# Gate matmuls, balancing rounds and attention spread out beside the products of a mixture-of-experts kernel

## The chip, the cores and the metric

The kernel runs on one core of a Trainium2 chip. The metric is the device time of one execution in microseconds (us). The core has five engines that run side by side, each with a queue of its own that it works off in order: TensorE (PE in the rows; its weight loads are PEld), VectorE (DVE), ScalarE (ACT), GpSimd (POOL) and SyncE (SP), which here only issues transfers. TensorE writes to PSUM, a memory of eight banks, which VectorE and ScalarE empty. Semaphores order the engines among each other. TensorE's clock has two levels, 1.2 and 2.4 GHz; the profile shows the granted share of the full one, 0.50 or 1.00.

## The reference

Three parts follow each other. `x` is 4 x 8 x 512 x 64, `state` 4 x 8 x 32 x 64; the tokens of both make N = 2176 rows of 512.

```python
# attention: x reads state, state reads x
a  = softmax(scale * x @ state.T);   xread = a @ state
a2 = softmax(scale * state @ x.T);   sread = a2 @ x
x  = concat([xread, sread], axis=2)  -> (2176, 512)

# first mixture of experts: all 8 experts for all rows, weights P balanced over rows and columns
logits = x @ w_gate
P = exp(logits - logits.max())
for _ in range(8):
    P /= P.sum(1) + 1e-9
    P /= P.sum(0) + 1e-9
    P *= N / E
out = sum over e of P[:, e:e+1] * (relu(x @ w1[e]) @ w2[e])      # w1[e] 512x1024, w2[e] 1024x512

# second: each row goes to one expert (argmax), scaled by its softmax weight and a sigmoid
```

The balancing needs the logits of all rows before its first round, and the expert sum needs its result, so the kernel of before already begins with unweighted sums.

## The kernel before

All of the change lies in the first two parts. The rows form 17 tiles of 128 (tiles 0 to 15 are `xread`, tile 16 is `sread`), and the products of the first mixture run in three passes of six, six and five tiles. A pass has 32 steps `s`: eight experts times four quarters of the hidden size (`FQ` = 256). A step is split in two halves. `mm1(s)` computes the hidden quarter for all tiles of the pass by seven block products of a fast matrix scheme (42 matmuls of 384 columns, since each value is split in a high and a low part and three partial products are taken). `mm2(s)` multiplies that with the second weights, tile by tile (six matmuls of 512 columns a tile), and adds the result to the tile's accumulator `acc` on VectorE. The program order on TensorE is mm1(0), mm1(1), mm2(0), mm1(2), mm2(1), and so on: `mm2(s-1)` stands behind `mm1(s)`.

The order of everything is written out by hand (`manual_schedule`). Batches 0 and 1 of attention are computed ahead of the first step, in a prologue. All other small work sits in a list, `queue`, of closures. Between the products `pump(dt)` adds `dt` (1.04 behind each of the seven block products, 1.36 behind each tile of `mm2`, about their time in us) to a credit, and takes the next item off the list each time the credit reaches `pace`. So `pace` is the distance between items in us of products, and an item's matmuls go into TensorE's queue at that place, its other instructions into the queues of their engines. `flush()` issues all that is left at once.

In the kernel of before the list holds, in this order: three gate batches for tiles 0 to 3, 4 and 5, 6 and 7; the items of batches 2 and 3 of attention (`window(2)`, `window(3)`, which also hold the state-reads-x part of batches 0 and 1, and end with a gate batch of four tiles each); the state-reads-x part of batches 2 and 3; the gate of tile 16. These 52 items have a pace of 66/52 = 1.27. Then `close_reads` releases attention's memory, sets the pace to 2.4, and the balancing follows: s0, s1, and eight rounds of two items, `row` and `col(i)`. At step 9 whatever is left is flushed and the routing constants are made on GpSimd. A gate of one tile is four matmuls with 8 columns (each two records in the trace, for the two halves of a 4-byte product), whose 128 x 128 stationary operand is the tile.

While the weights of the balancing aren't known, experts 0 and 1 are summed raw: expert 0 in `acc`, expert 1 in `xst` (the six tiles' transposed x, not needed any more by then). In the first quarter of expert 2 (`u == 2 * NQ`, `mm2(8)`, which stands in step 9's place behind mm1(9)) each tile's accumulator is scaled by its weight for expert 0, the raw sum of expert 1 is added with its weight, and the product of expert 2 with its own. From there on each eviction is one VectorE operation (`scalar_tensor_tensor`).

`load_x`, `load_state`: transfers of attention's inputs, the first on SyncE's queue, the second on ScalarE's, behind a memset on VectorE. `load_state(2)` and `load_state(3)` are issued just ahead of the first step, behind the splits of the first tiles. `state_T(b)` transposes the state of a batch on TensorE; it is the first item of `window(b)`. `prep_w1`, `prep_w2` split the next weights in high and low parts on ScalarE and GpSimd.

Lines of the kernel before that the rows below name: L137 `load_state`'s transfer, L166 `state_T`, L195, L206, L231, L243 attention's x-reads-state matmuls, L257, L272, L281 those of state-reads-x, L303 gate, L328 to L332 `row`, L337 to L341 `col`, L432 the low parts of the summed first weights, L465 to L467 `mm1`, L527 to L529 `mm2`, L541 and L542 the scaling and the merge of expert 1, L547 the weighted eviction.

Of the kernel before, what the change touches and what calls it, by code (L numbers as in the profile page):

```python
# [15 lines left out]
ALU = mybir.AluOpType  # L16
# [5 lines left out]
def tile_state_attention_moe_moe2(  # L22
# [13 lines left out]
    nc = tc.nc  # L36
    B, H, S, D = x.shape
    NS = state.shape[2]
    N, DM = out.shape
# [271 lines left out]
    def sinkhorn():  # L311
        steps = []
        mx, dg, ng = small([P, 1]), small([P, P]), small([P, 1])
        rs, rr = small([P, NT]), small([P, NT])
        cp, cr = small([P, E]), small([P, E])

        def s0():
            nc.vector.tensor_reduce(out=mx, in_=L1, axis=AX.XY, op=ALU.max)
            nc.vector.tensor_scalar_mul(dg, ident, mx)

        def s1():
            ps = bank("psmx")
            nc.tensor.matmul(ps[:, 0:P], ones, dg, start=True, stop=True)
            nc.vector.tensor_reduce(out=ng, in_=ps[:, 0:P], axis=AX.X, op=ALU.max, negate=True)
            nc.scalar.activation(out=PG, in_=L1, func=AF.Exp, bias=ng)

        def row():
            nc.vector.tensor_reduce(out=rs, in_=PG, axis=AX.X, op=ALU.add)  # L328
            nc.vector.tensor_scalar_add(rs, rs, EPS)
            nc.vector.reciprocal(rr, rs)  # L330
            nc.vector.tensor_tensor(out=PG, in0=PG, in1=rr.unsqueeze(2).to_broadcast([P, NT, E]), op=ALU.mult)
            nc.vector.tensor_reduce(out=cp, in_=PG.rearrange("p t e -> p e t"), axis=AX.X, op=ALU.add)  # L332

        def col(i):
            def f():
                ps = bank(f"pscol{i}")
                nc.tensor.matmul(ps[:, 0:E], ones, cp, start=True, stop=True)  # L337
                nc.vector.tensor_scalar_add(cr, ps[:, 0:E], EPS)
                nc.vector.reciprocal(cr, cr)
                nc.vector.tensor_scalar_mul(cr, cr, float(N) / E)  # L340
                nc.vector.tensor_tensor(out=PG, in0=PG, in1=cr.unsqueeze(1).to_broadcast([P, NT, E]), op=ALU.mult)  # L341
            return f

        steps += [s0, s1]
        for i in range(8):
            steps += [row, col(i)]
        return steps


# [166 lines left out]
    def accv(t):  # L516
        return acc[:, t % 6, :]

    def mm2(s, t):
        p, u = divmod(s, NU)  # L520
        e, q = divmod(u, NQ)
        hh, hl = hbuf(s)
        whi, wlo = W2[s]
        ps = bank(f"py{s}_{t}")
        r = slice((t - PASSES[p][0] // P) * P, (t - PASSES[p][0] // P + 1) * P)
        for j in range(2):
            nc.tensor.matmul(ps, hh[:, j, r], whi[:, j, :], start=(j == 0), stop=False)  # L527
            nc.tensor.matmul(ps, hh[:, j, r], wlo[:, j, :], start=False, stop=False)  # L528
            nc.tensor.matmul(ps, hl[:, j, r], whi[:, j, :], start=False, stop=(j == 1))  # L529
        a = accv(t)  # L530
        if p == 0 and e < 2:

            if e == 1:
                a = xst[:, t * DM : (t + 1) * DM]
            if q == 0:
                nc.vector.tensor_copy(a, ps)
            else:
                nc.vector.tensor_tensor(out=a, in0=ps, in1=a, op=ALU.add)
            return
        if p == 0 and u == 2 * NQ:  # L540
            nc.vector.tensor_scalar_mul(a, a, PG[:, t, 0:1])  # L541
            nc.vector.scalar_tensor_tensor(out=a, in0=xst[:, t * DM : (t + 1) * DM], scalar=PG[:, t, 1:2], in1=a,  # L542
                                           op0=ALU.mult, op1=ALU.add)
        if p > 0 and u == 0:
            nc.vector.tensor_scalar_mul(a, ps, PG[:, t, 0:1])
        else:
            nc.vector.scalar_tensor_tensor(out=a, in0=ps, scalar=PG[:, t, e : e + 1], in1=a, op0=ALU.mult, op1=ALU.add)  # L547
# [325 lines left out]
    with tc.manual_schedule():  # L873
# [57 lines left out]
        def flush():  # L931
            while queue:
                queue.pop(0)()
# [7 lines left out]
        def seq(*fs):  # L941
            def f():
                for g in fs:
                    g()
            return f

        def window(b):

            c, e = crit[b, 0], crit[b, 1]
            (n10, n20, n30), (n11, n21, n31) = lag[b - 2, 0], lag[b - 2, 1]  # L950

            def nx(g, f):
                def h():
                    f()
                    if b + 1 < B:
                        load_x(b + 1, g)
                    else:
                        load_x(b - 1, g)
                return h
            return [lambda: state_T(b), c[0], seq(lambda: load_x(b - 2, 0), n10), e[0], seq(lambda: load_x(b - 2, 1), n11),  # L960
                    c[1], n20, e[1], c[2], n21, e[2], c[3], nx(0, n30), e[3],
                    nx(1, n31), c[4], e[4], gate(range(4 * b, 4 * b + 4))]

        home = [None]

        def close_reads():
            actx.close()
            rtp[0] = ctx.enter_context(tc.tile_pool(name="rtp", bufs=1, side="right", reuse_waits="tile"))
            RT["oh"] = rtp[0].tile([P, NT, E], BF, name="oh")
            RT["bk"] = rtp[0].tile([P, NT], F32, name="bk")  # L970
            RT["g"] = rtp[0].tile([P, 2, NT], FR, name="gsplit")
            smp[0] = rtp[0]
            pace[0] = 2.4
            raw2 = ctx.enter_context(tc.tile_pool(name="raw2", bufs=1, side="right", reuse_waits="tile")).tile(
                [P, 4096], F32, name="raw2")
            R2[1], R2[2], R2[3] = raw2[:, 0:2048], raw2[:, 2048:4096], raw2[:, 0:2048]
            home[0] = raw2
            fin[0] = xctx.enter_context(tc.tile_pool(name="fin", bufs=2, side="right", reuse_waits="tile"))
            ohp[0] = xctx.enter_context(tc.tile_pool(name="ohp", bufs=1, side="right", reuse_waits="tile"))
# [39 lines left out]
                    f()  # L1019


        queue += [gate(range(0, 4)), gate(range(4, 6)), gate(range(6, 8))]
        for g in range(G):
            load_x(2, g)
        load_state(2)
        load_state(3)
        queue += window(2) + window(3)
        (a0, a1, a2), (b0, b1, b2) = lag[2, 0], lag[2, 1]
        queue += [a0, b0, a1, b1, seq(a2, lambda: load_x(3, 0)), seq(b2, lambda: load_x(3, 1))]
        (a0, a1, a2), (b0, b1, b2) = lag[3, 0], lag[3, 1]  # L1030
        queue += [a0, b0, a1, b1, a2, b2, seq(gate(range(NT - 1, NT)), states_out)]
        pace[0] = 66.0 / len(queue)
        queue += [close_reads] + sinkhorn()

        for s in range(3 * NU):
            p, u = divmod(s, NU)
            if s == 9:
                flush()
                routing_constants()
            if p < 2 and u == 14:  # L1040
                xload(p + 1)
            if p < 2 and u == 24:
                sums, T0 = xsums(p + 1, home[0])
                queue += sums
                pace[0] = 4.0
            if s == NU + 1:
                queue += list(Rq[0])
                pace[0] = 3.0
            if s == 2 * NU + 1:
                queue += [Rq[1][0], seq(Rq[1][1], sel_a), Rq[1][2], Rq[2][0], sel_b, sel_c, Rq[2][1], load_first, first_rows, Rq[2][2]]  # L1050
                pace[0] = 4.0
            step_mm1(s)
            if u < NU - 1:
                if u > 0:
                    step_mm2(s - 1)
                continue
            flush()
            ts = list(tiles_of(p))
            if p < 2:

                todo += xsplit(p + 1, T0)
                step_mm2(s - 1)
                hooks = {ts[i]: [A[ts[i - 1]]] + ([Bq[ts[i - 2]]] if i > 1 else []) for i in range(1, 6)}
                step_mm2(s, hooks)
                while todo:
                    todo.pop(0)()
                queue += [seq(A[ts[5]], Bq[ts[4]]), Bq[ts[5]]]
                pace[0] = 2.0
            else:
                load_first_raw(0, 0)  # L1070
                for i in (2, 3, 0, 1):
                    todo.append(lambda i=i: split_piece(SETS[0], i, 1024, nc.gpsimd))
                todo.append(lambda: load_first_raw(1, 1))
                step_mm2(s - 1)
                step_mm2(s, {13: [A[12]], 14: [A[13], Bq[12]], 15: [A[14], Bq[13]], 16: [Bq[14], A[15], lambda: xT(0)]})
# [142 lines left out]
```

## Time and profile before

| what | value |
|---|---|
| median of 3 runs (lowest to highest) | 1878.95 us (1878.01 to 1881.89) |
| the profiled execution: its time / its span | 1879.49 us / 1877.8 us |
| mean granted clock of TensorE | 0.973 |
| TensorE busy | 1804.5 us, 96% |
| VectorE / ScalarE / GpSimd busy | 65% / 35% / 59% |
| transfers | 154.65 MB, mean 82 GB/s |

Times of rows count from the span's start. A row of the timeline gives start, duration, engine, line, operation, output and inputs, the number of like instructions that follow each other, and in brackets the idle time of the engine before it with what ended it. Matmuls overlap, so the distance from one start to the next is the price of a matmul, not its duration. A row of the stretches gives the stretch and its length, the busy us (and instructions) of PE, PEld, DVE, ACT and POOL, the mean granted clock, the share of the transfer engines and GB/s. A row of the groups gives all instructions of a line and form.

### The profile page before, as it was taken

The numbers are of one execution on the slowest core, as the hardware profiler recorded it, in microseconds if no ns is written. First come the engines' busy times: TensorE is split into PE (matmuls) and PEld (weight loads), VectorE is DVE, ScalarE is ACT, GpSimd is POOL, SyncE is SP. The second block draws the span as 40 slices with busy tenths as digits, with TensorE's granted clock in tenths as the row PEclk, the third lists the DMA queues.
The fourth block names the chain that finished last, engine by engine and source line by source line (L and its number), as shares of the span: only waits on it lengthen the run. The fifth ranks groups of instructions, "written<-read, shape, count | busy, mean of one in ns | idle before, by whom it ended". The sixth has DMA issues, their size and how long they took to land.

```text
span 1877.8 us, 25502 instructions
## 1 busy us (share of the span) xinstructions
PE 1804.5 (96%) x9327; PEld 1607.7 (86%) x9327; DVE 1211.8 (65%) x2041; ACT 653.3 (35%) x1114; POOL 1099.3 (59%) x857
## 2 busy tenths in 40 slices
PE   7998899999999999999999999799999999899998
PEld 5997788999999889999999998689999899778886
DVE  5664769666666676666666666896666666745332
ACT  3432222333333333333333333333333343345333
POOL 2432456666776566666667765577787877412212
PEclk8799899999999999999999999899999999999999
DMA  4243112322222222222222222232222222245122
GB/s 113 74 107 96 51 45 68 102 68 68 68 68 68 90 80 71 70 71 96 68 68 68 68 67 84 67 129 81 80 79 79 90 79 68 76 137 199 62 81 89
DMA packets 126618, 154.65 MB, mean 82 GB/s; under 512 B 41424, under 2 KB 91600, under 8 KB 123920
## 3 DMA queue, kind: packets, MB, share of 16 engines
q1 hardware_dynamic: 121920, 142.41, 24.2%
q0 software_dynamic: 3280, 10.23, 1.7%
q8 instruction: 75, 1.23, 0.3%
q14 instruction: 63, 0.52, 0.1%
q10 hardware_dynamic: 1280, 0.26, 0.1%
HBM read 138.99 MB, written 14.42 MB: 82 GB/s over the span
## 4 chain that ended last, share of the span: by engine, by line
PE 74%; DVE 9%; issue 9%; DMA 5%; POOL 2%; ACT 1%; SPq 0%; POOLq 0%; DVEq 0%; ACTq 0%
PE py L527 12%; PE py L528 12%; PE py L529 12%; PE p L465 11%; PE p L467 11%; PE p L466 11%; DMA out_dram<-xst,si 4%; DMA out_dram<-y,si 1%; DVE HB L478 1%; PE psg L303 1%; PE psr L281 1%; PE pss L206 1%; PE pl L576 1%; DVE acc L547 1%; PE pso L243 1%
## 5 line engine op out<-in xcount | busy, mean ns | idle before, releaser
L443 POOL TENSOR_TENSOR wl<-rawb,wh 128x1024 fp32r<-128x1024 f32 x96 | 230.8, 2405 | 473.1 <-ACT wh L442 473.1
L465 PE MATMUL p<-XR 128*128 128x384 f32 (+1 forms) x1344 | 447.9, 333 | 4.2 <-ACT XR L390 2.8
L467 PE MATMUL p<-XR 128*128 128x384 f32 (+1 forms) x1344 | 444.1, 330 | 4.1 <-POOL XR L432 3.0
L466 PE MATMUL p<-XR 128*128 128x384 f32 (+1 forms) x1344 | 443.7, 330 | 0.9 <-DVE XR L392 0.9
L527 PE MATMUL py<-wh,HB 128*128 128x512 f32 x1088 | 431.6, 397 | 2.4 <-DVE acc L547 2.3
L528 PE MATMUL py<-wl,HB 128*128 128x512 f32 x1088 | 429.0, 394 | 0.0
L529 PE MATMUL py<-wh,HB 128*128 128x512 f32 x1088 | 428.6, 394 | 0.0
L547 DVE SCALAR_TENSOR_TENSOR acc<-py,PG,acc 128x512 f32<-128x512 f32 x485 | 338.9, 741 | 79.3 <-PE py L529 78.7
L432 POOL TENSOR_TENSOR XR<-sst,XR 128x1024 fp32r<-128x1024 f32 x96 | 255.0, 2656 | 50.8 <-ACT XR L426 50.8
L465 PEld LDWEIGHTS p<-XR 128*128 128x128 f32 x1344 | 256.8, 191 | 11.3 <-ACT XR L390 4.1
L467 PEld LDWEIGHTS p<-XR 128*128 128x128 f32 x1344 | 256.5, 191 | 5.4 <-POOL XR L432 3.8
L466 PEld LDWEIGHTS p<-XR 128*128 128x128 f32 x1344 | 256.7, 191 | 4.9 <-DVE XR L392 1.5
L478 DVE SCALAR_TENSOR_TENSOR HB<-u,HB 128x384 fp32r<-128x384 f32 (+1 forms) x192 | 169.3, 883 | 117.4 <-ACT HB L474 117.2
L529 PEld LDWEIGHTS py<-wh,HB 128*128 128x128 f32 x1088 | 206.7, 190 | 44.2
L527 PEld LDWEIGHTS py<-wh,HB 128*128 128x128 f32 x1088 | 206.8, 190 | 44.0 <-DVE acc L547 3.0
L528 PEld LDWEIGHTS py<-wl,HB 128*128 128x128 f32 x1088 | 206.6, 190 | 39.7
L483 ACT COPY u<-p 128x384 f32<-128x384 f32 (+1 forms) x96 | 44.3, 461 | 527.6 <-PE p L467 523.5
L428 POOL TENSOR_TENSOR XR<-rawb,XR 128x512 fp32r<-128x512 f32 x96 | 141.6, 1475 | 7.4 <-ACT XR L422 7.4
L426 ACT CAST XR<-sst 128x1024 fp32r<-128x1024 f32 x96 | 100.8, 1050 | 93.7 <-POOL sst L421 93.7
L474 ACT ACTIVATE HB<-u 128x384 fp32r<-128x384 f32 (+1 forms) x192 | 96.9, 505 | 80.0 <-DVE u L501 72.2
L486 DVE TENSOR_TENSOR u<-p,u 128x384 f32<-128x384 f32 (+1 forms) x96 | 51.3, 534 | 112.6 <-PE p L467 108.2
L474 ACT ACTIVATE HB<-p 128x384 fp32r<-128x384 f32 (+1 forms) x96 | 45.5, 474 | 190.4 <-PE p L467 190.4
(292 smaller groups left out, 2491.4 us busy)
## 6 DMA issues: line engine op xcount, KB each, us to landing
rawb<-in_moe_w_dram SPq DMA_DIRECT2D x192, 512.0 KB, 3.5
raw<-in_moe_w_dram SPq DMA_DIRECT2D x15, 1024.0 KB, 6.4
xb<-in_x_dram SPq DMA_DIRECT2D x60, 128.0 KB, 3.1
rawb<-in_moe_w_dram SPq DMA_DIRECT2D x5, 1024.0 KB, 5.1
x1d<-acc SPq DMA_DIRECT2D x16, 256.0 KB, 2.4
xtd<-xtm SPq DMA_DIRECT2D x4, 512.0 KB, 3.0
x1p<-acc SPq DMA_DIRECT2D x8, 256.0 KB, 2.6
xst<-xtd SPq DMA_DIRECT2D x1, 1536.0 KB, 8.3
```

Of the source, the lines that this page charges most:

```text
L428: nc.gpsimd.tensor_tensor(out=wop(s, 1, 0, 2).rearrange(r, k=KD), in0=raw[:, :, 0:P], in1=wop(s, 0, 0, 2).rearrange(r, k=KD).bitcast(F32), ...
L432: nc.gpsimd.tensor_tensor(out=wop(s, 1, 3, 4), in0=sst.rearrange("p a c -> p (a c)"), in1=wop(s, 0, 3, 4).bitcast(F32), op=ALU.subtract)
L443: nc.gpsimd.tensor_tensor(out=lo, in0=raw, in1=hi.bitcast(F32), op=ALU.subtract)
L465: nc.tensor.matmul(ps, wh, xh, start=start and k == 0, stop=False, skip_group_check=True)
L466: nc.tensor.matmul(ps, wh, xl, start=False, stop=False, skip_group_check=True)
L467: nc.tensor.matmul(ps, wl, xh, start=False, stop=stop and k == 1, skip_group_check=True)
L474: nc.scalar.activation(out=hh[:, f, half * h : (half + 1) * h], in_=c, func=AF.Relu)
L478: nc.vector.scalar_tensor_tensor(out=hl[:, f, q], in0=c, scalar=0.0, in1=hh[:, f, q].bitcast(F32), op0=ALU.max, op1=ALU.subtract)
L527: nc.tensor.matmul(ps, hh[:, j, r], whi[:, j, :], start=(j == 0), stop=False)
L528: nc.tensor.matmul(ps, hh[:, j, r], wlo[:, j, :], start=False, stop=False)
L529: nc.tensor.matmul(ps, hl[:, j, r], whi[:, j, :], start=False, stop=(j == 1))
L547: nc.vector.scalar_tensor_tensor(out=a, in0=ps, scalar=PG[:, t, e : e + 1], in1=a, op0=ALU.mult, op1=ALU.add)
```

## The change

- Gate: one tile at a time, and no longer in batches. `spread(fs, ts, n)` puts a gate behind every `n` items. Tiles 6, 7 and 0 to 5 go among the items of `window(2)` (two items, a gate), tiles 8 to 11 among those of `window(3)` (three items, a gate), 12 to 15 among the last twelve. The list begins with `state_T(2)`.
- Pace: 132 over the number of items (64: 25 + 21 + 16 and the last two) = 2.06 for attention and gate.
- Balancing: a round's `col` and the next round's `row` are one item; ten items in all. They are put in the list at step 9 (2 * NQ + 1), at the pace of 5.6 that `close_reads` now sets, and flushed at step 13.
- Raw experts: `NRAW` = 3. Expert 2 is summed raw in `home[0]`, the memory that `close_reads` takes over. In `mm2(12)` each accumulator is scaled and the product of expert 3 added. The raw sums of experts 1 and 2 are added by twelve `merge` items (one VectorE operation each) at a pace of 3.6 behind it, followed by the routing constants.
- The load of the next pass's tiles into `xst` starts in the 21st step of a pass, before in the 15th.

```diff
-        steps += [s0, s1]
-        for i in range(8):
-            steps += [row, col(i)]
+        steps += [s0, both(s1, row)]
+        for i in range(7):
+            steps.append(both(col(i), row))
+        steps.append(col(7))
...
+    NRAW = 3
+    home = [None]
+
+    def apart(e, t):
+        return (xst if e == 1 else home[0])[:, t * DM : (t + 1) * DM]
+
+    def merge(e, t):
+        a = accv(t)
+        return lambda: nc.vector.scalar_tensor_tensor(out=a, in0=apart(e, t), scalar=PG[:, t, e : e + 1], in1=a,
+                                                      op0=ALU.mult, op1=ALU.add)
...
-        if p == 0 and e < 2:
-
-            if e == 1:
-                a = xst[:, t * DM : (t + 1) * DM]
+        if p == 0 and e < NRAW:
+
+            if e > 0:
+                a = apart(e, t)
...
-        if p == 0 and u == 2 * NQ:
+        if p == 0 and u == NRAW * NQ:
             nc.vector.tensor_scalar_mul(a, a, PG[:, t, 0:1])
-            nc.vector.scalar_tensor_tensor(out=a, in0=xst[:, t * DM : (t + 1) * DM], scalar=PG[:, t, 1:2], in1=a,
-                                           op0=ALU.mult, op1=ALU.add)
...
-                    nx(1, n31), c[4], e[4], gate(range(4 * b, 4 * b + 4))]
+                    nx(1, n31), c[4], e[4]]
...
-            pace[0] = 2.4
+            pace[0] = 5.6
...
-        queue += [gate(range(0, 4)), gate(range(4, 6)), gate(range(6, 8))]
...
-        queue += window(2) + window(3)
+        def spread(fs, ts, n):
+
+            fs, out_ = list(fs), []
+            for t in ts:
+                out_ += fs[:n] + [gate([t])]
+                del fs[:n]
+            return out_ + fs
+
+        queue += spread(window(2), [6, 7, 0, 1, 2, 3, 4, 5], 2)
+        queue += spread(window(3), range(8, 12), 3)
         (a0, a1, a2), (b0, b1, b2) = lag[2, 0], lag[2, 1]
-        queue += [a0, b0, a1, b1, seq(a2, lambda: load_x(3, 0)), seq(b2, lambda: load_x(3, 1))]
-        (a0, a1, a2), (b0, b1, b2) = lag[3, 0], lag[3, 1]
-        queue += [a0, b0, a1, b1, a2, b2, seq(gate(range(NT - 1, NT)), states_out)]
-        pace[0] = 66.0 / len(queue)
-        queue += [close_reads] + sinkhorn()
+        (c0, c1, c2), (d0, d1, d2) = lag[3, 0], lag[3, 1]
+        queue += spread([a0, b0, a1, b1, seq(a2, lambda: load_x(3, 0)), seq(b2, lambda: load_x(3, 1)), c0, d0, c1, d1, c2, d2],
+                        range(12, 16), 2)
+        queue += [seq(gate([NT - 1]), states_out), close_reads]
+        pace[0] = 132.0 / len(queue)
+        balance = sinkhorn()
...
-            if s == 9:
-                flush()
-                routing_constants()
-            if p < 2 and u == 14:
+            if p < 2 and u == 20:
                 xload(p + 1)
...
             if u < NU - 1:
+                if s == 2 * NQ + 1:
+                    flush()
+                    queue += balance
+                if s == NRAW * NQ + 1:
+                    flush()
                 if u > 0:
                     step_mm2(s - 1)
+                if s == NRAW * NQ + 1:
+                    queue += [merge(e, t) for e in range(1, NRAW) for t in tiles_of(0)] + [routing_constants]
+                    pace[0] = 3.6
```

## Rows read from the trace of the kernel before

**Rows 1.** The page: busy time by engine, and the clock in 40 slices.

```profile
PE 1804.5 (96%) x9327; PEld 1607.7 (86%) x9327; DVE 1211.8 (65%) x2041; ACT 653.3 (35%) x1114; POOL 1099.3 (59%) x857
...
PEclk8799899999999999999999999899999999999999
```

**Rows 2.** Stretches: steps 0 to 1, 2 to 4, 5 to 7, 10, 18 to 28.

```profile
40.54:70.99 30.45, 28.25 (x116) 26.95 (x117) 16.15 (x23) 9.17 (x14) 12.58 (x10) 0.55 0.33 89
...
97.53:192.43 94.90, 89.78 (x543) 79.25 (x542) 54.65 (x104) 30.64 (x68) 30.09 (x24) 0.95 0.39 103
192.43:261.67 69.24, 58.01 (x253) 49.19 (x252) 55.49 (x123) 16.08 (x28) 29.38 (x24) 0.88 0.15 46
...
292.69:312.52 19.83, 16.34 (x80) 13.89 (x78) 18.37 (x25) 5.16 (x9) 10.83 (x8) 1.00 0.17 53
...
421.07:591.64 170.57, 170.57 (x860) 154.68 (x858) 113.48 (x176) 56.72 (x99) 122.63 (x92) 1.00 0.22 68
```

**Rows 3.** Timeline of the opening: TensorE, ScalarE's queue, GpSimd.

```profile
47.07 6.83 PE L303 MATMUL psg<-wg,xst 128*128 128x8 f32 x32
...
53.29 3.66 ACTq L137 DMA_DIRECT2D stp<-in_state_dram  x8
...
66.48 0.63 PE L166 MATMUL psst<-ident,stp 128*128 128x128 f32 x2
...
71.20 2.46 POOL L432 TENSOR_TENSOR XR<-sst,XR 128x1024 fp32r<-128x1024 f32 x1 [5.56 <-ACT XR L426]
```

**Rows 4.** Transfer issues: output and input, queue, count, KB each, us to landing.

```profile
stp<-in_state_dram ACTq DMA_DIRECT2D x16, 16.0 KB, 1.8
```

**Rows 5.** Stretches around gates and a balancing wait (the clock is third from last).

```profile
64.42:69.40 4.98, 4.98 (x17) 4.88 (x18) 1.86 (x5) 0.90 (x2) 1.22 (x2) 0.50 0.34 105
106.10:109.60 3.50, 3.50 (x34) 3.50 (x33) 0.79 (x2) 0.00 (x0) 3.21 (x4) 1.00 0.82 313
110.40:113.90 3.50, 3.50 (x13) 3.40 (x13) 1.36 (x4) 1.00 (x3) 0.00 (x0) 0.51 0.57 174
151.30:158.10 6.80, 6.80 (x27) 6.02 (x27) 1.21 (x3) 0.00 (x0) 0.00 (x0) 0.51 0.11 43
188.70:192.30 3.60, 3.60 (x21) 3.07 (x21) 1.55 (x3) 0.00 (x0) 0.00 (x0) 1.00 0.28 77
...
253.90:260.70 6.80, 6.41 (x16) 5.15 (x17) 3.42 (x9) 0.00 (x0) 0.00 (x0) 0.50 0.01 2
```

**Rows 6.** Timeline of TensorE: the gate of one tile, among products.

```profile
188.76 0.95 PE L303 MATMUL psg<-wg,xs 128*128 128x8 f32 x8
```

**Rows 7.** Groups of TensorE, 40 to 313 us: busy, mean ns, idle before.

```profile
L303 PE MATMUL psg<-wg,xtm 128*128 128x8 f32 x80 | 12.3, 291 | 0.4 <-DVE xtm L249 0.4
...
L272 PE MATMUL psb<-ident,e 128*128 128x128 f32 x32 | 4.9, 274 | 4.7 <-DVE e L266 4.7
...
L337 PE MATMUL pscol<-sm,ones 128*128 128x8 f32 x16 | 3.5, 293 | 11.2 <-DVE sm L332 11.2
L231 PE MATMUL psa<-ident,e 128*128 128x128 f32 x16 | 2.5, 276 | 0.9 <-DVE e L226 0.9
```

**Rows 8.** Timeline of TensorE: the longest wait among attention's last items.

```profile
180.58 0.63 PE L272 MATMUL psb<-ident,e 128*128 128x128 f32 x4 [3.63 <-DVE e L266]
```

**Rows 9.** Groups of VectorE, 192.43 to 261.67 us: the balancing's costliest and cheapest.

```profile
L340 DVE TENSOR_SCALAR sm<-sm 128x8 f32<-128x8 f32 x8 | 5.4, 670 | 0.3
...
L338 DVE TENSOR_SCALAR sm<-pscol 128x8 f32<-128x8 f32 x8 | 1.2, 155 | 0.1
```

**Rows 10.** One line's instructions, ns min/median/max: scaling, merge, weighted eviction.

```profile
L541 DVE TENSOR_SCALAR acc<-acc,PG x6: 477/708/2620, 288.3 to 302.9; 128x512 f32<-128x512 f32 x6
...
L542 DVE SCALAR_TENSOR_TENSOR acc<-xst,PG,acc x6: 751/929/1111, 290.9 to 303.6; 128x512 f32<-128x512 f32 x6
...
L547 DVE SCALAR_TENSOR_TENSOR acc<-py,PG,acc x485: 731/737/753, 291.8 to 1615.2; 128x512 f32<-128x512 f32 x162
```

More of the change, by code (lines that the diff above doesn't have):

```diff
@@ L342, in col, with both, h @@
             return f
-        steps += [s0, s1]
-        for i in range(8):
-            steps += [row, col(i)]
+        def both(f, g):
+            def h():
+                f()
+                g()
+            return h
+        steps += [s0, both(s1, row)]
+        for i in range(7):
+            steps.append(both(col(i), row))
+        steps.append(col(7))
         return steps
@@ L961, in window @@
                     c[1], n20, e[1], c[2], n21, e[2], c[3], nx(0, n30), e[3],
-                    nx(1, n31), c[4], e[4], gate(range(4 * b, 4 * b + 4))]
-        home = [None]
+                    nx(1, n31), c[4], e[4]]
         def close_reads():
```

## The prediction, made before the result was known

> **What bounds the kernel now.** I read the page first. TensorE is busy for 96% of the span, and its clock row is 9 nearly throughout, with dips in the first twelfth [rows 1]. So time can only come from three places: work taken off TensorE, its gaps, and its half-speed stretches. I then cut the span by steps of the first product stage (a step is one quarter expert: 42 products of 384 columns and 36 of 512) with the stretch view [rows 2]. Undisturbed, eleven steps take 170.57 us, 15.51 each, at clock 1.00, and no engine holds them up. The reader should compare the other stretches with that: steps 5 to 7, beside which the balancing rounds run, take 69.24 instead of 46.53; steps 2 to 4, beside attention, 94.90 instead of 46.53; step 10, where the gate weights are first applied, 19.83. From step 11 on the diff only moves the load of the next tiles, which keeps about 60 us of slack. Everything is decided between 40.5 and 312.5 us.
>
> Of the 272 us there, 162.4 are products at full speed (two first halves of a step and one second half, 50,688 columns in 22.8; then nine steps at 15.51). About 57 us are attention, gate and balancing matmuls, which the change moves and does not remove. The rest, some 52 us, is half gaps, half time lost to the half clock. That is the purse.
>
> **The change part by part.**
>
> *The opening (40.5 to 74 us).* Before, the queue starts with three gate batches over eight tiles. They run at the half clock in the first step, and the first alone takes 6.83 us [rows 3]. The new queue starts with the state transposes of batch 2, and its pace, 132 over 64 items = 2.06, pops them in the same place, behind the second product at 47.07. They need the state of batch 2, which comes from eight DMA issues on ScalarE's queue (53.29 to 56.95), behind the splits of the first tiles [rows 3]. Four belong to batch 2, the last issued near 55.1, and landing takes 1.8 us at the median [rows 4]. Nothing ahead of them moves, so TensorE, which works in order, stands from 47.1 to about 57. The gates were this gap's cover; in the row of before the same transposes come at 66.48 and wait for nothing. Behind them stand the products, and behind these the evictions.
>
> Then the clock: before, it returned at the end of 64.42 to 69.40, 5 us of products without a gate at 0.50 [rows 5]. Counting 5 to 6 us from 57, it is back near 62.5. Two products (2 us each at half speed) and eight transposes precede that, two products, one gate and one more product follow (1.03 us a product: 2304 columns of the 34,560 in 15.51 us), so step 1 starts near 67 instead of 71. There the second product waits for GpSimd's low parts, which end at 73.66 before [rows 3]; the ScalarE copy that releases them is queued behind the first step's activations, which now come 4 us earlier with the products, so I put the end near 70. So the kernel is 3.5 us ahead at that point, but owes seven gates that before had done by then: at 0.95 for eight matmuls of one tile, overlapping its neighbours a little [rows 6], I take 0.9, 6.3 in all. **−3 us** (a loss). Bounds: +1 if the clock rises earlier, −7 if it stays half to 69.4 as before.
>
> *Attention and the other gates (74 to 192 us, now to the end of step 9).* Gaps before: 4.7 behind the normalised exponentials, 0.9 and 0.4 at others [rows 7], 6.0 together. In the last attention items the dependent pairs stood two items apart at pace 1.27, 2.5 us, and the largest wait there lacked 3.63 [rows 8]; now they stand three apart at 2.06, 6.2 us, which just covers the 6.1. I leave 1.0. Clock: the batch of four gates (106.10 to 109.60) left the clock at 0.51 for 3.5 us right behind it, the next batch for 6.8 [rows 5]: 1.7 + 3.4 = 5.1 lost. The single gate inside 188.70 to 192.30 left it at 1.00 [rows 5]. All are single now; I leave 1.0. **+9.1** (0 to +11). The Trainium skill ("TensorE: Matmul & The Clock Gate", HAM oscillation) puts a fall of the clock down to idle gaps of TensorE. By that rule a batch without gaps would cost no clock and this term would be 5 and the time 1863. The trace disagrees: the stretch 106.10 to 109.60 is busy throughout and the fall follows it. A single gate also ends with a restart of the product stream, about 0.09 us: six more of them here, **−0.5**.
>
> *Balancing.* Before: 69.24 − 46.53 − 3.5 for the column sums' matmuls = 19.2 lost, 11.2 of them waits for the row sums, the rest clock (253.90 to 260.70 is one of three such stretches) [rows 2, 5, 7]. Each round was two items at pace 2.4; VectorE got only 2.4 us of products between a column's update and its row's. Now a round is one item every 5.6 us, and the chain of nine small operations follows its matmul directly. VectorE's side: those nine groups cost 26.9 us for eight rounds, 3.36 each (the costliest and the cheapest of the nine stand in [rows 9]), the products need 113.48/170.57 = 0.665 us of VectorE per us [rows 2], 3.73 in 5.6. That makes 7.1 a round, against 5.6 + 0.44 = 6.04 of TensorE. So VectorE falls behind by 1.05 a round; TensorE feels it once the backlog exceeds 6.04 − 3.36 = 2.7 us, after two or three rounds; four or five rounds then wait 1.05 each: 5 us. Three of the old waits were followed by a half-clock stretch; some rounds stay long, so one or two falls remain: 3. Lost 8 instead of 19.2: **+11.2**. Bounds: 0 (as before) to +18 (no wait).
>
> *Third expert apart.* Its raw sums use the same kind of eviction and cost nothing. In the first weighted step a tile had three VectorE operations, now two: a scaling, 0.71 median (up to 2.62), and the product's own, 0.74. Before, the step behind overran by 19.83 − 15.51 = 4.3 because three operations took 2.4 us a tile (0.71 + 0.93 + 0.74) against 1.38 of TensorE (3072 columns); now 1.45, with one long scaling. I leave 1: **+3.3** (0 to +4.3). The twelve merges, at 0.93 median of the same operation [rows 10], come to 11 us over three steps, where VectorE has 3 × (15.51 − 10.32) = 15.6 free. Behind a merge wait evictions, and TensorE has several PSUM banks in hand; nothing charged. The bound is 12 × 2.62 = 31.4, 16 us too many. The Trainium skill ("GPSIMD Engine Reference", Key points) says that VectorE operations with two SBUF inputs, which a merge is, contend with GpSimd for the SBUF interfaces. By the worst reading each merge waits a whole GpSimd operation, which is the second rival below; the rows [rows 10] lie between 0.75 and 1.11, so contention is there and small.
>
> Two hidden edits: the routing constants, GpSimd work that fell in steps 8 and 9 without a gap, do the same later; the load of the next tiles has four steps before its first reader.
>
> **Sum.** −3.0 + 9.1 − 0.5 + 11.2 + 3.3 = 20.1 us. Span 1877.8 − 20.1 = 1857.7; the profiled time lies 1.7 above its span and 0.5 above the median, so 1858.9 as a median, **1859**.
>
> **Rivals.**
>
> *All of the moved work is hidden.* No wait in balancing and no fall of the clock after the opening. For: VectorE's long rounds come from GpSimd, and in a lucky phase they vanish. Against: the 7.1 to 6.04 above. 20.1 + 8 + 3 + 1 = 32: 1847. Chance 0.13.
>
> *The merges wait for GpSimd.* 16 us of VectorE too many come back as TensorE's waits: 20.1 − 16 = 4, 1875. For: one operation of 2.62. Against: six merges of before, none above 1.11. Chance 0.06.
>
> *Balancing stays as it was.* VectorE-bound rounds with a fall of the clock in most: gain 20.1 − 11.2 = 9, 1870. For: VectorE's 7.1 us a round stays above TensorE's 6.0, so each round still ends in a wait. Chance 0.15.
>
> *Slower: each gate drops the clock.* Seventeen gates spread among products each leave 3.5 us at half speed, as the batch did, 1.7 lost: 29 instead of the 1 that I leave, 1859 + 28 = 1887. It decides from about twelve falls. For: in the opening, gates alternating with products held the clock at 0.55 on average over 30 us [rows 2]. Against: there the gates took most of the time, here 0.9 of about 7 us, and the one single gate of before left 1.00. Chance 0.08.
>
> **How the numbers follow.** The forecast (gain 13 to 27) has 0.58. The predicted time is its own. The range 1847 to 1871 takes in all-hidden and balancing-as-before at its ends and leaves out the merges and the slower case and half of the edges: about 0.2. What a measurement of this kernel can tell from no change is 0.2%, 3.8 us. Faster: 0.58 + 0.13 + 0.15 and part of the merges' case, 0.88; same 0.04; slower 0.08.
>
> **What would show it.** The opening: a TensorE gap of about 10 us ended by the state's DMA in the first step, and step 1 starting near 67. Attention: clock 1.00 from there to step 9 and no gap over 1 us. Balancing: waits for the row sums of 4 to 6 us instead of 11.2, with one or two half-clock stretches. Weights: the step behind the first weighted evictions under 17 us, and no waits for accumulators in the three after it. The forecast is wrong if the opening's gap is absent, if the clock falls behind single gates, or if the rounds wait as long as before.

## The result, and the profile after

| | before | changed |
|---|---|---|
| median, same chip (lowest to highest) | 1880.42 us (1878.01 to 1882.70) | 1862.46 us (1857.87 to 1865.07) |
| ratio, 95% interval | | 0.9902, 0.9878 to 0.9926 |
| profiled execution: time / span | 1879.49 / 1877.8 us | 1862.84 / 1861.1 us |

The change makes the kernel 18.0 us faster by the medians and 18.4 by the ratio; 20 were forecast. The profiled spans differ by 16.7. The fence holds the stretches of the changed kernel that answer to [rows 2]: steps 0 and 1; attention and gates to the end of step 8; steps 9 to 12, beside which the balancing now runs; step 13, undisturbed; step 14, behind the first weighted evictions. To compare: the first row of [rows 2], 30.45 us, is step 0 alone; steps 0 and 1 of the kernel before end at 97.53 us and take 56.99.

```profile
41.17:90.72 49.55, 36.72 (x206) 32.77 (x207) 35.69 (x54) 19.32 (x33) 25.73 (x19) 0.83 0.38 98
70.20:244.86 174.66, 174.66 (x1052) 157.51 (x1050) 122.08 (x219) 62.32 (x126) 81.26 (x64) 1.00 0.33 92
244.86:321.82 76.96, 69.94 (x332) 61.72 (x332) 64.70 (x140) 21.14 (x37) 39.81 (x32) 0.93 0.17 55
321.82:337.33 15.51, 15.51 (x80) 14.06 (x78) 11.06 (x15) 5.16 (x9) 10.49 (x8) 1.00 0.21 68
337.33:356.62 19.29, 17.40 (x80) 15.11 (x79) 18.12 (x24) 5.15 (x9) 11.62 (x8) 0.91 0.19 56
```

The second row is the clearest. For 175 us TensorE is busy without a gap at full clock, though attention and sixteen gates run through it. What TensorE lost in each part, gaps and half clock together, from half-microsecond stretches of both kernels (busy time times the missing share of the clock, plus idle time):

| part | before | changed | gain | forecast |
|---|---|---|---|---|
| opening, to the low parts' end (73.7 / 70.2) | 2.8 + 12.8 | 12.8 + 3.2 | −0.4 (−2 as the forecast counts: 4.4 us earlier, seven gates of 0.9 owed) | −3 |
| attention and gates | 6.0 + 5.1 | 0 + 0 | +11.1 | +9.1 − 0.5 |
| balancing (steps 5 to 7 / 9 to 12) | 11.2 + 7.9 | 7.0 + 4.7 | +7.4 | +11.2 |
| overrun behind the first weighted evictions | 4.3 | 3.8, and 0.3 in step 16 | +0.2 | +3.3 |

The gains sum to 18.3 us. The first product starts 0.6 later, which leaves the 17.6 by which step 17 starts earlier. Steps 17 to 30 take 15.51 each in both kernels. Step 31, where the pass changes, takes 38.02 instead of 36.88; in the kernels below it varies between 35.1 and 38.1, also where the edit doesn't touch it.

The groups of TensorE, changed kernel, 40 to 357 us, answer to [rows 7] (last columns: busy, mean ns, idle before and what ended it).

```profile
L303 PE MATMUL psg<-wg,xtm 128*128 128x8 f32 x80 | 9.5, 245 | 0.0
...
L272 PE MATMUL psb<-ident,e 128*128 128x128 f32 x32 | 4.8, 272 | 0.0
...
L337 PE MATMUL pscol<-sm,ones 128*128 128x8 f32 x16 | 3.1, 266 | 6.5 <-DVE sm L332 6.4
L231 PE MATMUL psa<-ident,e 128*128 128x128 f32 x16 | 2.4, 272 | 0.0
L166 PE MATMUL psst<-ident,stp 128*128 128x128 f32 x4 | 1.0, 352 | 9.1 <-DMA stp<-in_state_dram 9.1
```

Attention's waits are gone, those for the row sums are down from 11.2 to 6.4, and a new one stands in the last row. The opening in the timeline and in stretches, changed kernel (answers to [rows 3, 5]):

```profile
57.05 0.66 PE L166 MATMUL psst<-ident,stp 128*128 128x128 f32 x2 [9.14 <-DMA stp<-in_state_dram]
...
66.65 2.66 POOL L440 TENSOR_TENSOR XR<-sst,XR 128x1024 fp32r<-128x1024 f32 x1
...
69.36 0.44 PE L475 MATMUL p<-XR 128*128 128x384 f32 x1 [1.56 <-POOL XR L440]
```

```profile
47.90:57.00 9.10, 0.00 (x1) 0.00 (x0) 5.32 (x6) 3.13 (x4) 3.65 (x2) 0.50 0.09 19
57.05:59.60 2.55, 2.55 (x9) 2.55 (x10) 0.89 (x2) 1.97 (x4) 0.47 (x1) 0.50 0.10 23
```

TensorE stands 9.14 us for the state's transfer. The clock is at 0.50 throughout, and for another 2.55 us of transposes and products; from 59.8 us on it is full.

Behind the first weighted evictions, VectorE and TensorE, changed kernel:

```profile
343.11 0.75 DVE L564 SCALAR_TENSOR_TENSOR acc<-py,PG,acc 128x512 f32<-128x512 f32 x1
343.77 5.15 DVE L535 SCALAR_TENSOR_TENSOR acc<-xst,PG,acc 128x512 f32<-128x512 f32 x4
348.85 0.54 DVE L494 TENSOR_TENSOR u<-p,u 128x384 f32<-128x384 f32 x1
...
349.44 0.50 PE L546 MATMUL py<-wh,HB 128*128 128x512 f32 x1 [1.89 <-DVE u L494]
```

Four merges run in one piece (5.15 us), the evictions of the next products (L494) stand behind them, and TensorE waits 1.89 us for a PSUM bank. In the whole set a merge takes more than before ([rows 10]):

```profile
L535 DVE SCALAR_TENSOR_TENSOR acc<-xst,PG,acc x6: 736/1202/1754, 343.8 to 357.7; 128x512 f32<-128x512 f32 x6
L535 DVE SCALAR_TENSOR_TENSOR acc<-raw,PG,acc x6: 733/1285/2393, 360.4 to 379.9; 128x512 f32<-128x512 f32 x6
```

Three of the eight column sums wait, for 2.77, 1.10 and 2.53 us. Here are the two longest waits (last line of each part), with the VectorE operation that was held up ahead of them and the GpSimd operation beside it:

```profile
273.09 2.40 POOL L440 TENSOR_TENSOR XR<-sst,XR 128x1024 fp32r<-128x1024 f32 x1 [1.52 <-ACT XR L434]
273.47 2.43 DVE L486 SCALAR_TENSOR_TENSOR HB<-u,HB 128x384 fp32r<-128x384 f32 x1 [0.55 <-ACT HB L482]
...
279.00 0.60 PE L337 MATMUL pscol<-sm,ones 128*128 128x8 f32 x2 [2.77 <-DVE sm L332]
...
312.30 2.36 POOL L440 TENSOR_TENSOR XR<-sst,XR 128x1024 fp32r<-128x1024 f32 x1 [1.19 <-ACT XR L434]
...
312.74 1.95 DVE L329 TENSOR_SCALAR sm<-sm 128x17 f32<-128x17 f32 x1
...
315.80 0.60 PE L337 MATMUL pscol<-sm,ones 128*128 128x8 f32 x2 [2.53 <-DVE sm L332]
```

In the first, it is an operation of the products (L486, on the hidden values, 0.55 us elsewhere) that takes 2.43; in the second, an operation of the round itself on 17 columns (L329, 0.18 elsewhere) that takes 1.95. Both end within 0.5 us of GpSimd's operation. The wait of 1.10 stands behind an L486 of 2.44. A held operation need not cost a wait: another L329 took 1.99, and the column sum behind it waited 0.09.

### The profile page after: what moved, and what is told of

The parts are those of the page before. It is cut to its first block, busy times and chain, and to the rows that moved or that the text cites. A ratio compares the mean times of both kernels' runs of the same rounds, so it can differ in the third digit from the quotient of the medians.

```text
span 1861.1 us, 25503 instructions
## 1 busy us (share of the span) xinstructions
PE 1789.1 (96%) x9327; PEld 1594.7 (86%) x9327; DVE 1229.1 (66%) x2058; ACT 654.0 (35%) x1114; POOL 1101.3 (59%) x857
## 4 chain that ended last, share of the span: by engine, by line
PE 75%; issue 11%; DVE 7%; DMA 4%; POOL 2%; ACT 1%; SPq 0%; POOLq 0%; DVEq 0%; ACTq 0%
PE py L546 12%; PE py L547 12%; PE py L548 12%; PE p L473 11%; PE p L475 11%; PE p L474 11%; DMA out_dram<-xst,si 2%; DMA out_dram<-y,si 1%; PE pss L206 1%; DVE HB L486 1%; PE pl L593 1%; PE psg L303 1%; PE psr L281 1%; POOL XR L440 1%; PE pso L243 1%
## 5 line engine op out<-in xcount | busy, mean ns | idle before, releaser
L564 DVE SCALAR_TENSOR_TENSOR acc<-py,PG,acc 128x512 f32<-128x512 f32 x461 | 321.7, 741 | 73.1 <-PE py L548 72.5
L486 DVE SCALAR_TENSOR_TENSOR HB<-u,HB 128x384 fp32r<-128x384 f32 (+1 forms) x192 | 180.5, 941 | 114.3 <-ACT HB L482 114.0
L494 DVE TENSOR_TENSOR u<-p,u 128x384 f32<-128x384 f32 (+1 forms) x96 | 51.2, 534 | 107.4 <-PE p L475 100.1
```

What stands on the lines that cost most here:

```text
L486: nc.vector.scalar_tensor_tensor(out=hl[:, f, q], in0=c, scalar=0.0, in1=hh[:, f, q].bitcast(F32), op0=ALU.max, op1=ALU.subtract)
```

## The experiments

Each line of results gives the ratio to the kernel before on the same chip with its 95% interval; the changed kernel has 0.9902. Times by step come from the profiled execution, where runs agree in undisturbed steps to 0.01 us, so they tell apart what the ratios alone don't. The changes of pass don't agree like that (step 31 above; step 62 takes 32.3 to 35.6), so the whole time of a single profile says less than its steps.

**States early** (`e1_state_early`, on the changed kernel).

```diff
-        stp = ap2.tile([P, G, P], F32, tag="stp", name=f"stp{b}")
+        stp = ap2.tile([P, G, P], F32, tag="stp", name=f"stp{b}", bufs=4)
...
         load_x(1, 1)
+        load_state(2, nc.sync)
+        load_state(3, nc.sync)
         A1[0]()
```

> The changed kernel, with the states of batches 2 and 3 fetched into buffers of their own on SyncE's queue in the prologue, and no longer on ScalarE's queue behind the splits of the first tiles. Theory: the 9.14 us that TensorE stands for the state's transfer in the first step go, the clock comes back a few us earlier, and the low parts of the next weights on GpSimd become the wait, 3 to 6 us; gain over the changed kernel 4 to 7 us. Rival A: the gap only hides the same GpSimd chain, which doesn't move: gain under 2. Rival B: nothing else is late: gain 9 and more.

Measured: 1856.20 us, 0.9865 (0.9848 to 0.9881). Steps 0 and 1 take 46.32 us instead of 49.55, and step 2 begins 5.3 earlier (2.0 of that lie ahead of the first product, whose start varies from 39.1 to 42.8 between these kernels, so 3.2 are sure). TensorE's waits in the opening of this kernel:

```profile
52.06 0.44 PE L473 MATMUL p<-XR 128*128 128x384 f32 x1 [1.73 <-ACT u L491]
60.65 0.60 PE L475 MATMUL p<-XR 128*128 128x384 f32 x1 [3.92 <-POOL XR L436]
```

The gap of 9.14 goes and half of it comes back as waits for ScalarE and for GpSimd's low parts. The theory holds in kind. The 3.2 us that are sure lie a little under its 4 to 7 and over Rival A's 2; the ratios would say 7.0, more than the opening accounts for.

**Merges one by one** (`e2_merge_credit`, on the changed kernel).

```diff
-                    pace[0] = 3.6
+                    pace[0], credit[0] = 3.6, 0.0
```

> The changed kernel, with the credit set to zero when the twelve merges are put in the list, so that they start one by one and not with those that the saved credit pays for at once. Theory: the step behind the first weighted evictions (19.29 us) is long because five merges in a row hold up the eviction behind them: it falls to 15.5 to 16.5 and its half-clock stretch goes, gain 3 to 4 us. Rival: the merges are slow because they wait for GpSimd (their sum is what counts, not their order): the step stays over 18, or the 3 us turn up in the next two steps.

Measured: 1856.95 us, 0.9862 (0.9846 to 0.9879). Step 14 takes 15.50 us instead of 19.29, step 15 15.51, step 16 15.51 instead of 15.80:

```profile
336.41:351.91 15.50, 15.50 (x79) 14.06 (x78) 14.98 (x22) 5.16 (x9) 10.48 (x8) 1.00 0.22 69
351.91:367.42 15.51, 15.51 (x79) 14.06 (x78) 15.34 (x22) 5.26 (x9) 11.16 (x8) 1.00 0.22 68
```

VectorE is 97% to 99% busy there, single merges still take up to 2.87 us, and TensorE feels nothing. So it is the burst that costs, and not the merges' own length: had they been slow only, the step would have stayed long. Steps 14 to 16 gain 4.1 us. The mechanism: `pump` saves up to four items' worth of credit while the list is empty, and a list filled then starts with up to four at once.

**Rounds 6.8 us apart** (`e3_round_pace`, on the changed kernel): `pace[0] = 6.8` instead of 5.6 in `close_reads`.

> The changed kernel, with 6.8 us of products between balancing rounds in place of 5.6. Theory: VectorE's demand of about 7.1 us a round sets the waits, so with 6.8 + 0.4 of TensorE a round fits: waits for the row sums fall from 6.4 to under 2 us, and at most one half-clock stretch stays; gain 4 to 8 us. Rival: the long rounds come from single operations that are held up beside GpSimd, and hit whatever the pace: waits stay at 4 to 6 us and two half-clock stretches too, gain under 2.

Measured: 1857.68 us, 0.9874 (0.9857 to 0.9890). The waits stay at 5.7, as the rival said; the half-clock stretches all go, where the theory left at most one and the rival two:

```profile
246.50:332.75 86.25, 80.57 (x410) 72.30 (x410) 75.35 (x153) 26.24 (x46) 49.25 (x40) 1.00 0.20 62
```

Steps 9 to 13 take 86.25 us instead of 92.47; step 14 takes 21.68 instead of 19.29. The three waits (1.10, 3.13, 1.45) each end a round in which an operation was held beside GpSimd (an L329 of 1.97; an L486 of 2.43 and an L329 of 2.15; an L486 of 2.43), so the rival is right on their cause. The longest of them:

```profile
293.26 2.43 DVE L486 SCALAR_TENSOR_TENSOR HB<-u,HB 128x384 fp32r<-128x384 f32 x1 [0.61 <-ACT HB L482]
...
298.70 2.15 DVE L329 TENSOR_SCALAR sm<-sm 128x17 f32<-128x17 f32 x1
...
302.14 0.39 PE L337 MATMUL pscol<-sm,ones 128*128 128x8 f32 x2 [3.13 <-DVE sm L332]
```

My arithmetic was wrong too: a wider pace also lets more products' evictions into a round, and the nine groups took 26.4 us here. With these 3.30 a round VectorE would fit, by the mean, from a pace p with 0.335 p + 0.44 = 3.30 (0.335 us of VectorE are left free by each us of products, and 0.44 us is the column sum's own time on TensorE), which is 8.5 and not 6.8.

**Two batches of four gates again** (`e4_gate_batches`, on the changed kernel).

```diff
-        queue += spread(window(3), range(8, 12), 3)
+        w3 = window(3)
+        queue += w3[:3] + [gate(range(8, 12))] + w3[3:]
...
+        queue += [a0, b0, gate(range(12, 16)), a1, b1, seq(a2, ...), seq(b2, ...), c0, d0, c1, d1, c2, d2]
...
+        pace[0] = 132.0 / 64
```

> The changed kernel, with the gates of tiles 8 to 11 and of 12 to 15 as two batches of four again, at the place of their first single one; all other items and the pace as changed. Theory: each batch (3.5 us of matmuls with 8 columns) is followed by a half-clock stretch as before, of 3.4 to 6.8 us: 3 to 5 us longer than the changed kernel. Rival (the clock falls behind gaps only, and the batches have none): no half-clock stretch, and up to 0.5 us shorter since six restarts of the product stream go.

Measured: 1873.71 us, 0.9955 (0.9938 to 0.9972), 10 us slower than the changed kernel. Two half-speed stretches of 3.4 us are back, one in the step of each batch, 1.7 lost in each; a wait of 1.4 for an exponential comes with them. TensorE has no gap over 0.3 us from 70 to 224 us, and both falls (at 145.8 and 200.4) lie in that stretch, 0.5 to 1.2 us behind the end of their batches. To the start of step 9 the kernel is 4.9 us behind, as expected. What follows I had not foreseen: six fewer items empty the list earlier, credit is saved, and the balancing's first items start at once (the first two matmuls of the balancing have no product between them), with these waits (groups of TensorE, 249 to 285 us):

```profile
L337 PE MATMUL pscol<-sm,ones 128*128 128x8 f32 x8 | 1.7, 285 | 2.7 <-DVE sm L332 2.7
L323 PE MATMUL psmx<-sm,ones 128*128 128x128 f32 x2 | 0.8, 502 | 4.5 <-DVE sm L319 4.5
```

Step 9 takes 26.83 us here and 16.62 in the changed kernel, where its first wait is 0.52. Steps 12 and 14 give 3.9 and 1.6 back, which leaves 11 us in the profile and 10 by the ratios. No run has these batches without the saved credit.

**Single gates alone, on the kernel before** (`e5_gates_alone`): `spread` for the gates; pace 66 over the number of items, balancing and raw experts as before.

> The kernel before, with its gates one tile at a time at the places that the change gives them, and nothing else of the change: 66 us for attention, rounds of two items at 2.4, two raw experts, merge as before. Theory: the two half-clock stretches behind the batches (5.1 us) go, the opening loses about 2 us to the state's transfer, the waits in attention and balancing stay: 1 to 6 us faster than before, that is at most a third of the change's 17. Rival: the clock behind the batches was all of the gain: 12 us and more.

Measured: 1871.33 us, 0.9949 (0.9933 to 0.9966), 9.6 us less than before: half of the change, more than expected and less than the rival. From the first product to step 5 it gains 5.5 us, with the 9.28 us gap in its opening; attention's waits fall from 6.0 to 1.9, probably since a gate between two dependent items sets them apart (3 × 1.05 us against 2 × 1.27), which I had not counted. Another 2.5 lie in the balancing, whose waits grow (13.0) while its half-clock loss falls from 7.9 to 3.4; why was not tested.

**No saved credit anywhere** (`e6_no_saved_credit`, on the changed kernel).

```diff
                 queue.pop(0)()
+            if not queue:
+                credit[0] = 0.0
```

> The changed kernel, with the pump's credit set to zero whenever the list is empty, everywhere and not only at the merges. Theory: items put in an empty list were issued two to five at once; apart from the step behind the first weighted evictions (3.5 us) this makes the waits for the routing's one-hot rows at the start of passes 2 and 3 (about 4 us, 3.4 and 4.6 by the rows of before): gain over the changed kernel 8 to 14 us. Rival: those waits are the length of the VectorE chain itself and only move: gain of 3 to 5, as with the merges alone.

Measured: 1857.94 us, 0.9883 (0.9866 to 0.9899): the rival's gain. The wait of 4.07 us at the start of pass 2 goes (step 32: 29.36 instead of 32.35, step 14: 15.51). In pass 3 the chain is longer than the time it now has: steps 63 to 67 take 98.6 us instead of 93.6, with a wait of 5.35 for the routing's sums. The same edit helps and harms by place.

**Time split the other way** (`e7_split`, on the changed kernel): 110 us for attention instead of 132, the balancing straight behind it, 8.4 us a round.

```diff
-        pace[0] = 132.0 / len(queue)
-        balance = sinkhorn()
+        pace[0] = 110.0 / len(queue)
+        queue += sinkhorn()
...
-            pace[0] = 5.6
+            pace[0] = 8.4
```

> The changed kernel, with attention at 110 us instead of 132 and the balancing straight behind it at 8.4 us a round instead of 5.6. Theory: attention had no gap at 2.06 us an item and has at most 1 us at 1.72; a round of 8.4 us outlasts VectorE's 7 with its held operations, so the waits for row sums (6.9 us with the 0.5 of the first) fall to 2 and the clock's 4.7 go: gain 7 to 10 us over the changed kernel. Rival: waits come from single held operations at any pace, as at 6.8, where 5.7 us stayed: gain 3 to 5, from the clock alone.

Measured: 1851.12 us, 0.9840 (0.9824 to 0.9856), 11.7 us below the changed kernel by the ratios. Attention still has no gap; the steps beside the balancing (from step 8 on):

```profile
227.00:329.50 102.50, 100.61 (x506) 89.81 (x505) 89.84 (x174) 31.46 (x55) 59.12 (x48) 1.00 0.20 62
```

The waits for row sums are 1.1 us and the clock never falls: the balancing costs little more than its matmuls. Operations are still held (the nine groups take 29.5 us here, 23.7 in the changed kernel), and VectorE is busy 88% of this stretch, 84% of the changed kernel's steps 9 to 12. So neither the holds nor the load have gone; a round of 8.4 us has room for them. The edit also starts the balancing 14 us earlier; no run has rounds of 8.4 us at the old place.

**Seven small operations a round** (`e11_fewer_small_ops`, on the changed kernel, pace 5.6).

```diff
+        nc.vector.memset(onesE, float(E) / N)
...
-            nc.vector.tensor_scalar_add(rs, rs, EPS)
...
-                nc.tensor.matmul(ps[:, 0:E], ones, cp, start=True, stop=True)
-                nc.vector.tensor_scalar_add(cr, ps[:, 0:E], EPS)
+                nc.tensor.matmul(ps[:, 0:E], onesE, cp, start=True, stop=True)
+                nc.vector.tensor_scalar_add(cr, ps[:, 0:E], EPS * E / N)
...
-                nc.vector.tensor_scalar_mul(cr, cr, float(N) / E)
```

> The changed kernel, with seven small VectorE operations a balancing round in place of nine: the factor N/E sits in the matrix that sums the columns, and the row sums go without the 1e-9. The pace stays 5.6. Theory: the demand on VectorE falls by those two groups (0.25 and 0.67 us a round by the rows of before), from 7.1 to about 6.2, close to TensorE's 6.0: waits for row sums fall from 6.9 to 1 to 3 us, gain 4 to 8 us. Rival: what is held beside GpSimd is whatever operation comes next, so the hold moves on to the neighbour and only 0.4 us a round goes: waits stay at 4 to 6, gain under 3.

Measured: 1857.51 us, 0.9879 (0.9860 to 0.9898). Waits for row sums 3.8 us instead of 6.4; steps 9 to 12 take 71.2 instead of 77.0. That is between the two. The gain, 5.8 us, is the theory's. But the rival is right on the hold: the two groups that went had taken 7.4 us, while the seven left take 20.0 against 23.7 for nine, 0.5 less a round, since in the two rounds where an L329 was held an operation behind it is held instead (1.99 and 1.83 us in place of 0.48 and 0.30). The group of that operation, here and in the changed kernel:

```profile
L332 DVE TENSOR_TENSOR PG<-PG,sm 128x136 f32<-128x136 f32 x8 | 6.1, 763 | 0.3
...
L331 DVE TENSOR_TENSOR PG<-PG,sm 128x136 f32<-128x136 f32 x8 | 2.9, 369 | 0.3
```

**Together.** `e8_all` is states early, no saved credit and the split; `e9_best` takes the credit away at the merges only; `e10_best_pass2` also where the routing's first items enter the list in pass 2 (`pace[0], credit[0] = 3.0, 0.0`).

> States early, no saved credit, and 110 us for attention with 8.4 us a round, together on the changed kernel. Theory: the parts add up: 5 + 10 + 8 = 20 to 25 us below the changed kernel. Rival: they share VectorE's idle time and give back part: 12 to 16.

> States early, the credit set to zero at the merges only, 110 us for attention and 8.4 us a round, on the changed kernel. Theory: the three gains of single runs lie in different stretches and add up: 5 (opening) + 3 (step behind the first weighted evictions, 17.5 and 16.65 at 8.4 us a round) below the 1851 of the split alone, so 1843, a ratio to before of about 0.980. Rival: an earlier opening only moves the wait to GpSimd's low parts and the merges still collide: 1848 to 1851.

> The same, with the credit also set to zero where the routing's first items enter the list in pass 2. Theory: the wait of 4.07 us for the one-hot rows goes, as it did with no credit saved anywhere, and pass 3 is left as it is: 2 to 4 us below the kernel without it. Rival: the items land on weighted evictions a step later (a wait of 2.06 for an accumulator there): within 1 us of it.

| kernel | median us | ratio to before |
|---|---|---|
| e8_all | 1850.04 | 0.9829 (0.9813 to 0.9846) |
| e9_best | 1846.90 | 0.9811 (0.9797 to 0.9826) |
| e10_best_pass2 | 1845.69 | 0.9804 (0.9788 to 0.9819) |

With no saved credit anywhere the sum falls to what its rival said; step 33 then waits 2.06 for an accumulator and pass 3 loses as above. With credit taken away at the merges alone steps 14 to 17 are all at 15.50 to 15.51. e9 lies between its two theories: its steps 14 and 15 gain the 3 us, but steps 0 and 1 take 49.12 us against 50.77 with the split alone, so the earlier opening gains 1.7 there and not 5. The last edit takes the 4.07 wait away (2.10 for low parts in its place), but the two medians lie 1.2 us apart with overlapping intervals: not told apart. By the ratios they are 17 and 18 us faster than the changed kernel.

## Why the prediction was right, step by step

*The sum and the sign* hold: 18.0 us by the medians against 20. That the sum came so near is in part luck: errors of 4 (balancing) and 3 (third expert) meet 2.5 the other way in attention and 2.6 in the opening (1 as the forecast counts it). The measured 1862 also lies next to the 1863 that the prediction works out for batches without a cost in clock; that is chance, since attention's term measured 11.1 and not 5.

*The opening.* Right in place and size: a gap of 9.14 us ended by the state's transfer (about 10 forecast), the low parts' wait at 69.36 against 73.71, 4.4 earlier (3.5 forecast). The clock came back at 59.8 and not near 62.5; step 1 starts at 65.6 and not near 67. States early shows that half of the gap was cover for GpSimd's chain.

*Attention and gates.* Right, and more than forecast: neither a gap nor a fall of the clock is left. Batches of four put the half-speed stretches back, one behind each, so the clock's share is shown. The Trainium skill ("TensorE: Matmul & The Clock Gate", HAM oscillation) puts a fall of the clock down to idle gaps of TensorE; that does not account for these falls either, since the batches have no gap. The slower rival is out: seventeen single gates at full clock, and the next fall comes 33 us behind the last of them. In one reading the prediction was loose: the 6.8 us at half clock that it puts behind the second batch begin inside it, at 151.4 (the batch lasts from 148.39 to 153.76); the sum is the same.

*Balancing.* The mechanism was right, the size of two terms was not: "four or five rounds then wait 1.05 each: 5 us" measured 6.4, and "one or two falls remain: 3" measured 4.7, so the gain is 7.4 instead of 11.2. What failed is the mean as the cause. The nine groups cost 23.7 us, 2.96 a round and not 3.36, so the mean was too high and the wait still too low: the waits come in three single rounds, behind an operation that is held beside GpSimd for about 2 us, and in two of the three that is an operation of the products. A wait of 2.5 us cost clock as well. That it is VectorE's chain that TensorE waits for is shown by seven operations, which shorten each of the three waits (to 1.60, 0.48 and 1.72), and by rounds of 8.4 us, which outlast a held operation (1.1 of waits in all).

*The third expert.* Wrong by 3 us: "Behind a merge wait evictions, and TensorE has several PSUM banks in hand; nothing charged" failed. I took the merges at their pace of 3.6 and did not follow the credit, which issued four at once; one edit of one number shows it (19.29 to 15.50). The rival in which the merges wait for GpSimd is out: one by one they still take up to 2.87 us, and steps 14 and 15 take 15.50 and 15.51.

*The later load of the next tiles* costs nothing, as forecast: steps 17 to 30 are alike, and step 31 takes 35.30 in the kernel with the credit taken away at the merges, which has the load at the same place.

## What to carry to other kernels

Where small work is paced among products, follow the pacing counter itself: what it has saved when a list is refilled is issued as a burst, and the burst, not the mean, makes the wait. Divide time between two paced chains by what each needs beside its cover: attention had none to lose at 1.72 us an item, and the balancing, once its rounds had 8.4 us, cost almost nothing. Size a round so that it outlasts its longest held operation, here some 2 us more than the mean says. When filler is moved, look at what it covered: here the gates stood over a transfer that nobody waited for.

## What the hardware showed that I had not expected

- A VectorE operation on 17 columns took 1.95 us instead of 0.18, and one on 384 columns 2.43 instead of 0.55; both ended within 0.5 us of the GpSimd operation beside them. Merges of 512 columns took 0.73 to 2.39.
- After 9.1 us without a matmul the clock was still at 0.50 for 2.55 us of matmuls and full from 59.8, 2.7 us behind the first of them; in the kernel before 4.98 us of products, with gates ahead of them, were at 0.50 throughout [rows 5].
- Waits of 2.5 us and more before a column sum were followed by a half-clock stretch in the changed kernel; waits of up to 3.1 us at the wider pace were not, up to step 13. What decides between them is open.
